# Strassen operands summed from the operand ring, stores on another queue, last products and softmax reordered

## The chip, the cores and the metric

The kernel runs on one core of one Trainium2 chip. The metric is the device time of one execution in microseconds (us); times of several executions are given by their median. PE is the matrix engine (TensorE), DVE the vector engine, ACT the scalar engine, POOL is GpSimd, and SP is the engine that issues most DMAs. Each engine takes its own instructions strictly in the order in which the program wrote them; semaphores hold an instruction back until what it needs is there.

## The reference

Three layers follow each other. First, linear attention with random features:

```
proj = x @ omega.T ;  phi(x) = exp(proj - |x|^2/2 - max) / sqrt(m)
num = phi(q) @ (phi(k).T @ v) ;  out = num / (phi(q) @ sum(phi(k)) + 1e-6)
```

Its output, as x of 2304 tokens by 512, goes into a dense mixture of four experts with given weights p: `out += p[:, e] * (relu(x @ w1[e]) @ w2[e])`, with w1[e] 512 x 1024 and w2[e] 1024 x 512. Last comes a soft mixture with 32 slots (8 experts of 4): logits `x @ phi`, a softmax over the tokens for each slot, `slot_input = d.T @ x`, two small layers for each expert, then a softmax over the slots for each token (`c`), and `out = c @ slot_out`. All is float32 to the accuracy of float32, so the kernel splits each operand into a high part (type fp32r) and a rest, and makes three products of each: high times high, high times rest, rest times high.

## The kernel before

**The dense mixture.** Its two layers are run in 24 *units*, u = 0 to 23: eight weight groups (four experts, two halves of the hidden width), each over three blocks of 768 tokens (b = u mod 3). A unit's first layer is a 2 x 2 block product. Units 0 to 2 do it plainly, in eight products (`plain1`); units 3 to 23 do it in Strassen's form with seven (`product1`, in the order I1 I2 I6 I5 I7 I3 I4). The second layer is always in Strassen's form (`product2`, seven products). A product of the first layer and one of the second alternate on PE: `product1(u, I1)`, `product2(u-1, I1)`, `product1(u, I2)`, and so on. One such product with all that is written after it is a *piece*.

**The operands.** The attention leaves x as high part and rest in DRAM (`xd`). The units take their x operands through a ring of three tiles (`xop`): `next_operand` (L457) loads the third one ahead as soon as a product is done with a tile. Strassen's form needs, for each block b, four operands that are not blocks of x but sums of such blocks (I6, I5, I7, I4). They are made once for each block and kept in DRAM (`xt`, lines 461 to 511):

- `fetch` loads high parts and rests of half a block from `xd`: four DMAs of 384 KB on SP's queue;
- `whole_again` (L472) adds the two, `block_sum` (L478) makes the four sums in place, all on DVE;
- `block_split` (L485, L487) copies the high part on ACT and subtracts it on DVE; two ticks later `keep` (L490, L491) writes both to `xt`, two DMAs on SP's queue.

`prepare(b)` puts the 18 steps of a block on a list, and every piece takes one from it (`prep_one`). Block 0 begins with unit 1, block 1 with unit 2, block 2 with unit 3, each behind what is left of the one before.

**The work between the products.** `evacuate1` takes a first-layer product out of PSUM (`u1`, `u2`, `u4`, `s1` are temporary tiles) and makes the second layer's operands, high (`split_high`, `corner_high` on ACT) and rest (`split_low` L587, `corner_low` L517 on DVE). `after(d, ...)` defers such a step to the d-th following `tick`, one of which ends each piece. For unit 23 (`hurry`) all delays from I3 on are 0. `evacuate2` adds the products of the second layer (L781) and collects them with the weights p into `x2` (L718, L720), one x2 tile for each block of tokens.

**The end.** The last group is cut into parts: letter q is a second-layer product for four of the six token tiles, r one for the other two, P a first-layer product. `SPLIT` (units 22, 23) and `ENDING` give their order; t is a task of the slot layer for a batch of four tiles: transposes (`tpm`), logits (`lq`), their sum over four partition groups and the exponentials (`slot_sum`: `lt`, L987), transposes back (`slot_back`: `dp`), `slot_gather` (`acc`), and the softmax over the slots (`slot_share1`, `slot_share2`, L1050 to L1061). During `SPLIT` each piece also takes one task off the list `side`. Behind `ENDING` the last batch is done in the open, then the hidden layer (`hq`), the second layer (`so`) and the output (`po`). The weights of the slot layer, 32 loads of 1 MB, stream in during all this; each load waits until the buffers that its place lay under are free, and the last ten take the places of the first ten.

Of the kernel before, what the change touches and what calls it, by code (L numbers as in the profile page):

```python
# [9 lines left out]
F32 = mybir.dt.float32  # L10
# [6 lines left out]
P = 128  # L17
# [23 lines left out]
def f32(ap):  # L41
    return ap.bitcast(F32)
# [3 lines left out]
def body(ctx: ExitStack, tc: tile.TileContext, ql, kl, vl, om, dp, wl, phi, w2l, out):  # L46
# [398 lines left out]
    whole = {I1: (0, 0), I2: (1, 0), I3: (1, 1)}  # L445

    def load_operand(u, i):
        b = units[u][1]
        x = xop.tile([P, 2, NP, 2 * P], F32R, name="x", tag="x")
        k = whole.get(i, i)  # L450
# [9 lines left out]

    def fetch(b, half):
        a = prep.tile([P, 2, 2 * TH], F32, name=f"xr{half}", tag=f"pre{half}")
        lo = prep.tile([P, 2, 2 * TH], F32, name="xl", tag="pre2")
        for k in range(2):
            src = xd[b][half][:, k]
            nc.sync.dma_start(out=three(a[:, k]), in_=f32(src[:, 0]))
            nc.sync.dma_start(out=three(lo[:, k]), in_=f32(src[:, 1]))
            blocks[b, (k, half)] = a[:, k], lo[:, k]
# [26 lines left out]
    prep_work = []  # L495

    def prepare(b):
        for half in range(2):
            prep_work.append(lambda half=half: fetch(b, half))
            prep_work.append(None)  # L500
            prep_work.extend(lambda kh=(k, half): whole_again(b, kh) for k in range(2))
        prep_work.extend(lambda n=n: block_sum(b, n) for n in range(4))
        for pair_ in ((I6, I5), (I7, I4)):
            prep_work.extend(lambda i=i: block_split(b, i) for i in pair_)
            prep_work.append(None)

    def prep_one():
        if prep_work:
            f = prep_work.pop(0)
            if f:  # L510
                f()

# [25 lines left out]
    def product1(u, i):  # L538
        if i in (I1, I2, I7):
            accumulator1("X" if i == I1 else "B")  # L540
        q = acc1["B" if i in (I2, I7, I4) else "X"][:, :, 0:TH]
        pass1(u, i, xs_.pop((u, i)), q, i in (I1, I2, I7))
        evacuate1(u, i, q)
        next_operand(u, i)
        weights_after(u, i)
        if u == XB and i == I1:
            prepare(u - 1)
        prep_one()
        tick()
        pump()  # L550

    def plain1(u, n):
        out = n // 2
        a, half = ((0, 0), (1, 0), (1, 1), (0, 1))[out]
        key = "XB"[out % 2]
        if n % 2 == 0:
            accumulator1(key)
        q = acc1[key][:, :, 0:TH]
        k = n % 2
        w = next(i for i, at in PLAIN.items() if at == (a, k))  # L560
        pass1(u, w, xs_[u, (k, half)], q, k == 0)
        if n in (2, 3, 6, 7):
# [6 lines left out]
        if u and n == 0:  # L569
            prepare(u - 1)  # L570
        prep_one()
        tick()
        pump()
# [23 lines left out]
    def evacuate1(u, i, q, plain=False):  # L597
# [8 lines left out]
        if u == 0:  # L606
            done.update(rd(i) for i in range(7))
        hurry = u == NU - 1
        now = (lambda n: 0) if hurry else (lambda n: n)

# [31 lines left out]
        elif i == I3:  # L642
# [7 lines left out]
            after(1, ("s2", u), second)  # L650
            after(now(1), ("h", u, I7), lambda: split_high(u, I7, q), rd(I7))
            after(now(1), ("h", u, I5), lambda: split_high(u, I5, s1), rd(I5))
# [15 lines left out]
    def rest(u, now=lambda n: n):  # L668
        L = lt_
# [5 lines left out]
        if units[u][0] == 0:  # L675
            after(1, ("s4", u), lambda: nc.vector.tensor_tensor(out=s4, in0=s4, in1=s2, op=ALU.subtract), ("s2", u))
        after(now(1), ("h", u, I6), lambda: split_high(u, I6, s2), ("s2", u), rd(I6))
        after(now(2), ("l", u, I6), lambda: split_low(u, I6, s2), ("h", u, I6))
        after(now(2), ("h", u, I3), lambda: split_high(u, I3, s4), ("s4", u), rd(I3))
        after(now(3), ("l", u, I5), lambda: split_low(u, I5, s1), ("h", u, I5))  # L680
        after(now(3), ("h", u, I4), lambda: split_high(u, I4, r22), ("r22", u), rd(I4))
        after(now(5), ("l", u, I3), lambda: split_low(u, I3, s4), ("h", u, I3))
        after(now(7), ("l", u, I4), lambda: split_low(u, I4, r22), ("h", u, I4))

# [37 lines left out]
    def product2(u, i, ps=range(NP), tags=None):  # L722
# [211 lines left out]
    def slot_tasks(b):  # L934
# [406 lines left out]
```

## Time and profile before

| | |
|---|---|
| three runs | median 1014.27 us (1012.26 to 1014.7) |
| profiled execution | 1012.07 us, of which the span from first to last instruction is 1010.2 us |
| PE busy | 960.0 us (95%) |
| DVE, ACT, POOL busy | 703.4, 502.1, 344.0 us (70%, 50%, 34%) |
| DMA on SP's queue | 231.54 MB, 66.7% of the 16 engines' span |
| mean granted clock of PE | 0.978 |

Busy shares are means over stages with different limits. A clock of 1.00 is 2.4 GHz, the lower level is 1.2 GHz; a stretch with both shows a value between. An instruction's idle time carries the name of what ended it.

### The profile page before, as it was taken

The numbers are of one execution on the slowest core, as the hardware profiler recorded it, in microseconds if no ns is written. First come the engines' busy times: TensorE is split into PE (matmuls) and PEld (weight loads), VectorE is DVE, ScalarE is ACT, GpSimd is POOL, SyncE is SP. The second block draws the span as 40 slices with busy tenths as digits, with TensorE's granted clock in tenths as the row PEclk, the third lists the DMA queues.
The fourth block names the chain that finished last, engine by engine and source line by source line (L and its number), as shares of the span: only waits on it lengthen the run. The fifth ranks groups of instructions, "written<-read, shape, count | busy, mean of one in ns | idle before, by whom it ended". The sixth has DMA issues, their size and how long they took to land.

```text
span 1010.2 us, 18116 instructions
## 1 busy us (share of the span) xinstructions
PE 960.0 (95%) x7074; PEld 914.8 (91%) x7074; DVE 703.4 (70%) x1268; ACT 502.1 (50%) x940; POOL 344.0 (34%) x288
## 2 busy tenths in 40 slices
PE   8999989997688999999999999999999999898797
PEld 8999989997688999999999999999999998786544
DVE  7888874888597767877676787667678665646422
ACT  5899883453443544445354444535544443343322
POOL 7888853142422341334134133414413240000000
PEclk9999999999799999999999999999999999797999
DMA  8688755776778565786656566665656654348995
GB/s 291 181 250 275 247 179 160 278 259 256 270 256 294 187 227 187 272 270 230 230 187 230 188 230 223 193 229 186 226 188 228 223 176 154 97 157 315 409 373 235
DMA packets 65525, 233.48 MB, mean 231 GB/s; under 512 B 8608, under 2 KB 17952, under 8 KB 61344
## 3 DMA queue, kind: packets, MB, share of 16 engines
q1 hardware_dynamic: 65152, 231.54, 66.7%
q8 instruction: 56, 0.92, 0.4%
q10 hardware_dynamic: 288, 0.79, 0.2%
q14 instruction: 29, 0.24, 0.1%
HBM read 208.71 MB, written 23.59 MB: 230 GB/s over the span
## 4 chain that ended last, share of the span: by engine, by line
PE 82%; DVE 8%; DMA 4%; ACT 3%; issue 1%; SPq 1%; ACTq 0%; POOL 0%; DVEq 0%
PE X L530 18%; PE X L738 16%; PE B L530 13%; PE B L738 12%; PE kv L220 3%; PE num L244 3%; PE Xq L738 2%; PE pj L176 2%; PE so L1201 2%; PE hq L1173 2%; PE pj L177 2%; PE pj L178 2%; PE tp L234 1%; PE Bq L738 1%; DMA xt<-xh 1%
## 5 line engine op out<-in xcount | busy, mean ns | idle before, releaser
L530 PE MATMUL X<-x,w1h 128*128 128x384 f32 x768 | 200.7, 342 | 15.1 <-ACT u L614 9.4
L530 PE MATMUL B<-x,w1h 128*128 128x384 f32 x600 | 154.2, 337 | 4.7 <-issue 2.9
L530 PEld LDWEIGHTS X<-x,w1h 128*128 128x128 f32 x768 | 137.4, 193 | 19.4 <-ACT u L614 9.8
L530 PE MATMUL X<-x,w1l 128*128 128x384 f32 x384 | 130.6, 340 | 0.0
L415 POOL TENSOR_TENSOR Tw<-raww 128x512 f32<-128x512 f32 x30 | 44.7, 1513 | 203.2 <-DMA raww<-wl 203.2
L530 PEld LDWEIGHTS B<-x,w1h 128*128 128x128 f32 x600 | 104.9, 189 | 6.2 <-issue 4.0
L530 PE MATMUL B<-x,w1l 128*128 128x384 f32 x300 | 100.4, 335 | 0.0
L601 DVE TENSOR_TENSOR u<-B,u 128x768 f32<-128x768 f32 x23 | 22.0, 957 | 101.7 <-PE B L530 101.7
L201 ACT ACTIVATE fe<-pj,nb 128x128 f32<-128x128 f32 x288 | 82.8, 389 | 10.1 <-DVE nb L194 9.3
L530 PEld LDWEIGHTS X<-x,w1l 128*128 128x128 f32 x384 | 73.6, 192 | 0.0
L429 POOL TENSOR_TENSOR w1l<-Tw,w1h 128x512 fp32r<-128x512 f32 x28 | 37.2, 1330 | 82.8 <-ACT w1h L428 82.8
L429 POOL TENSOR_TENSOR w2l<-raww,w2h 128x512 fp32r<-128x512 f32 x24 | 31.0, 1295 | 93.2 <-ACT w2h L428 93.2
L184 DVE TENSOR_REDUCE stat<-pj 128x4 f32<-128x512 f32 x72 | 49.5, 687 | 10.4 <-PE pj L178 9.6
L530 PEld LDWEIGHTS B<-x,w1l 128*128 128x128 f32 x300 | 56.3, 188 | 0.0
L429 POOL TENSOR_TENSOR w2l<-Tw,w2h 128x512 fp32r<-128x512 f32 x32 | 41.8, 1306 | 40.7 <-ACT w2h L428 40.7
L429 POOL TENSOR_TENSOR w1l<-raww,w1h 128x512 fp32r<-128x512 f32 x25 | 39.1, 1564 | 42.9 <-ACT w1h L428 42.9
L151 POOL TENSOR_TENSOR lo<-raw,hi 128x512 fp32r<-128x512 f32 x35 | 44.7, 1277 | 20.5 <-ACT hi L148 19.9
L583 ACT CAST s3h<-X 128x768 fp32r<-128x768 f32 x21 | 16.8, 802 | 67.8 <-DVE X L517 67.8
L176 PE MATMUL pj<-om_hi,hi 128*128 128x256 f32 x144 | 45.3, 315 | 1.4 <-ACT fe L201 1.1
L720 DVE SCALAR_TENSOR_TENSOR x<-B,pr,x 128x256 f32<-128x256 f32 x108 | 45.6, 478 | 1.3
L785 ACT COPY v<-X 128x768 f32<-128x768 f32 x42 | 33.7, 801 | 18.5 <-PE X L738 18.4
L178 PE MATMUL pj<-om_hi,lo 128*128 128x256 f32 x144 | 40.7, 282 | 0.8 <-POOL lo L151 0.8
(295 smaller groups left out, 3053.0 us busy)
## 6 DMA issues: line engine op xcount, KB each, us to landing
x<-xt SPq DMA_DIRECT2D x84, 768.0 KB, 4.3
x<-xd SPq DMA_DIRECT2D x75, 768.0 KB, 4.5
raww<-wl SPq DMA_DIRECT2D x16, 1024.0 KB, 7.1
w2tb<-w2l SPq DMA_DIRECT2D x11, 1024.0 KB, 8.5
raw<-ql SPq DMA_DIRECT2D x18, 512.0 KB, 4.4
xd<-xst SPq DMA_DIRECT2D x36, 256.0 KB, 2.9
raw<-kl SPq DMA_DIRECT2D x16, 512.0 KB, 5.0
w2ta<-w2l SPq DMA_DIRECT2D x5, 1024.0 KB, 6.9
```

Source lines behind the costliest of these rows:

```text
L151: (nc.gpsimd if i else nc.vector).tensor_tensor(out=lo, in0=r, in1=f32(hi), op=ALU.subtract)
L176: nc.tensor.matmul(o, lhsT=hi[:, pi, :], rhs=om_hi, start=True, stop=False)
L178: nc.tensor.matmul(o, lhsT=lo[:, pi, :], rhs=om_hi, start=False, stop=True)
L184: nc.vector.tensor_reduce(out=stats(i)[:, 4 * g:4 * g + 4, 0], in_=pjs[i, g], axis=AX.X, op=ALU.max)
L201: nc.scalar.activation(out=feats[i][:, 4 * g + h, :], in_=pjs[i, g][:, h, :], func=AF.Exp, bias=biases[i, g][:, h:h + 1], scale=1.0,)
L220: nc.tensor.matmul(kvps[b][h // 4][:, h % 4, :], lhsT=feats[i][p0:p0 + np_, h, :], rhs=v[p0:p0 + np_, h, :], start=first and h % 4 == 0, s ...
L415: nc.gpsimd.tensor_tensor(out=out_, in0=a, in1=b_, op=op)
L429: nc.gpsimd.tensor_tensor(out=lo, in0=src, in1=f32(hi), op=ALU.subtract)
L530: nc.tensor.matmul(o, lhsT=lhs[:, jp, c], rhs=rhs[:, :, k, :], start=first and not k and not n, stop=False, skip_group_check=True,)
L720: nc.vector.scalar_tensor_tensor(out=o, in0=src, scalar=w, in1=o, op0=ALU.mult, op1=ALU.add)
L738: nc.tensor.matmul(q[:, n, :], lhsT=lhs[:, jp, p, :], rhs=rhs[:, jp, :], start=i in (I1, I2, I7) and n % 2 == 0 and jp == 0 and m == 0, st ...
L785: nc.scalar.copy(out=v("v1"), in_=q)
```

## The change

Block 0 of x is still loaded from `xd`, but once, ahead of unit 1, all eight DMAs together, with the rests in the place where an x2 tile will lie. Blocks 1 and 2 are no longer loaded a second time: `whole` adds high part and rest directly from the ring's tiles while units 1 and 2 have them there. The stores to `xt` are issued by ACT. The steps stand in fixed slots: (u, 2i) is the piece of a first-layer product of unit u, (u, 2i+1) the second-layer product that follows it.

```diff
-    def fetch(b, half):
...
-    def whole_again(b, kh):
...
+    def fetch():
+        t = x2p.tile([P, 4, 2 * TH], F32, name="xl", tag="x2_1")
+        for n, (k, half) in enumerate(KH):
+            place(0, (k, half))
+            src = xd[0][half][:, k]
+            nc.sync.dma_start(out=three(blocks[0, (k, half)]), in_=f32(src[:, 0]))
+            nc.sync.dma_start(out=three(t[:, n]), in_=f32(src[:, 1]))
+            lows[k, half] = t[:, n]
...
+    def whole(b, kh):
+        if b:
+            place(b, kh)
+            hi, lo = xs_[b, kh]
+            out = three(blocks[b, kh])
+            nc.vector.tensor_tensor(out=out, in0=f32(hi), in1=f32(lo), op=ALU.add)
+        else:
+            a = blocks[b, kh]
+            nc.vector.tensor_tensor(out=a, in0=a, in1=lows[kh], op=ALU.add)
...
         def keep():
-            nc.sync.dma_start(out=f32(xt[b][i][:, 0]), in_=three(f32(hi)))
-            nc.sync.dma_start(out=f32(xt[b][i][:, 1]), in_=three(src))
+            nc.scalar.dma_start(out=f32(xt[b][i][:, 0]), in_=three(f32(hi)))
+            nc.scalar.dma_start(out=f32(xt[b][i][:, 1]), in_=three(src))
...
+        unit1 = [
+            (W, 1, KH[0]), (W, 0, KH[0]), (W, 1, KH[1]), (W, 0, KH[1]), (W, 0, KH[2]), (W, 0, KH[3]), (T, 0, 0),
+            (T, 0, 1), (W, 1, KH[2]), (T, 0, 2), (W, 1, KH[3]), (T, 0, 3), (S, 0, I5), (S, 0, I4),
+        ]
+        unit2 = [
+            (T, 1, 0), (T, 1, 1), (S, 0, I6), (S, 0, I7), (W, 2, KH[0]), (W, 2, KH[1]), (T, 1, 2), (T, 1, 3),
+            (S, 1, I6), (S, 1, I4), (W, 2, KH[2]), None, (W, 2, KH[3]), (S, 1, I5), (S, 1, I7),
+        ]
+        unit3 = [
+            None, None, *((T, 2, n) for n in range(4)), (S, 2, I6), (S, 2, I5), None, None, None,
+            (S, 2, I7), (S, 2, I4),
+        ]
```

In units 22 and 23 the steps behind I3 and I4 are deferred further (`late_` is true there, d = 1), and unit 23 has no `hurry` any more:

```diff
-            after(now(1), ("l", u, I7), lambda: split_low(u, I7, q), ("h", u, I7))
+            if not late_:
+                after(1, ("l", u, I7), lambda: split_low(u, I7, q), ("h", u, I7))
...
-            after(0, ("l", u, I2), lambda: corner_low(u, I2, q), ("h", u, I2))
-            after(0, ("s4", u), lambda: plus(pair(L["u2"]), q, pair(L["s2"]), ALU.subtract), ("s2", u))
-            rest(u, now)
+            after(2 * late_, ("l", u, I2), lambda: corner_low(u, I2, q), ("h", u, I2))
+            after(3 * late_, ("s4", u), lambda: plus(pair(L["u2"]), q, pair(L["s2"]), ALU.subtract), ("s2", u))
+            if late_:
+                x = acc1["X"][:, :, 0:TH]
+                after(3, ("l", u, I7), lambda: split_low(u, I7, x), ("h", u, I7))
+            rest(u, late_)
...
-        after(now(2), ("l", u, I6), lambda: split_low(u, I6, s2), ("h", u, I6))
+        after(2 + 2 * d, ("l", u, I6), lambda: split_low(u, I6, s2), ("h", u, I6))
```

The slot layer's tasks and the end:

```diff
-    ENDING = "q1 t q2 t q6 r1 t q5 t r2 t q7 q3 t r6 t q4 t r5 t t r7 t r3 t t r4 t t"
+    ENDING = "q1 t t q2 t q6 t q5 t q7 t q3 t q4 t t r1 r2 r6 t r5 r7 t r3 t r4"
...
-                turns[0:2], turns[2:], [], [logits], [], [total], [], [back, share1], [], [], [gather, share2],
+            tasks = [turns[0:2], turns[2:], [], [logits], [total], [], [back], [], [gather], [share1], [share2]]
...
-            tasks = [turns[0:2], turns[2:], [logits], [total], [], [back, share1], [], [gather, share2]]
+            tasks = [turns[0:2], turns[2:], [logits], [total], [], [back], [gather]]
         else:
-            tasks = [turns[0:2], turns[2:], [], [logits], [], [total]]
+            tasks = [turns[0:2], turns[2:], [logits], [total]]
...
+    slot_logits(n)
     slot_back(n - 1)
-    slot_logits(n)
+    keep_warm(4)
+    slot_sum(n)
     slot_gather(n - 1)
-    slot_sum(n)
-    slot_share1(n - 1)
-    slot_share2(n - 1)
+    keep_warm(6)
     keep_warm(10)
...
-    slot_share1(n)
-    slot_share2(n)
+    for b in (n - 2, n - 1, n):
+        slot_share1(b)
+        slot_share2(b)
```

The list `order`, which says which place each of the last layer's weights takes, is permuted: b10, c0, b9, c1, c2 come ahead of b0, b1, b2, b6.

## Rows read from the trace of the kernel before

**Rows 1.** The page: PE's busy tenths in 40 slices of the span
```profile
PE   8999989997688999999999999999999999898797
```
**Rows 2.** Stretches, one for each unit 1 to 6: length, busy us, clock, DMA share, GB/s
```profile
174.66:206.37 31.71, 31.71 (x224) 31.71 (x223) 26.43 (x33) 11.99 (x16) 8.86 (x9) 1.00 0.80 266
206.37:242.56 36.19, 33.55 (x224) 33.35 (x224) 27.06 (x36) 14.54 (x21) 10.45 (x7) 0.95 0.73 265
242.56:286.45 43.89, 32.85 (x211) 32.31 (x211) 31.71 (x36) 18.20 (x26) 13.73 (x9) 0.88 0.79 285
286.45:323.28 36.83, 30.76 (x211) 29.81 (x211) 30.48 (x40) 15.62 (x22) 6.88 (x5) 1.00 0.74 269
323.28:354.51 31.23, 31.23 (x211) 31.23 (x211) 23.46 (x33) 15.76 (x23) 13.13 (x10) 0.95 0.58 190
354.51:384.14 29.63, 29.63 (x212) 29.63 (x211) 21.22 (x29) 14.49 (x21) 12.55 (x10) 1.00 0.66 222
```
**Rows 3.** PE's waits, 206 to 330 us: total, times, longest
```profile
PE X L530 <- ACT u L614: 9.4, 2, 7.8
PE B L530 <- issue: 2.9, 1, 2.9
...
PE X L530 <- DMA x<-xd: 2.6, 1, 2.6
```
**Rows 4.** Waits of SP's queue, same stretch
```profile
SPq L490 <- ACT xh L485: 25.8, 7, 5.6
...
SPq L491 <- DVE xr L487: 13.2, 11, 2.9
```
**Rows 5.** DVE by line, 175 to 323 us: the operands' preparation
```profile
L472 DVE TENSOR_TENSOR xr<-xr,xl 128x768 f32<-128x768 f32 x12 | 14.3, 1191 | 13.2 <-DMA xl<-xd 11.6 <-issue 1.5
L487 DVE TENSOR_TENSOR xr<-xr,xh 128x768 fp32r<-128x768 f32 x12 | 14.0, 1166 | 9.8 <-ACT xh L485 9.5
```
**Rows 6.** Timeline of DVE and ACT in unit 3: start, length
```profile
256.01 2.04 DVE L587 TENSOR_TENSOR s1l<-s,s1h 128x768 fp32r<-128x768 f32 x1
...
264.42 0.95 DVE L587 TENSOR_TENSOR s4l<-u,s4h 128x768 fp32r<-128x768 f32 x1
...
265.46 0.80 ACT L614 COPY u<-X 128x768 f32<-128x768 f32 x1 [4.24 <-DVE s4l L587]
```
**Rows 7.** Timeline of ACT's queue: a DMA that it issues
```profile
1002.31 0.38 ACTq L1237 DMA_DIRECT2D out<-ob  x1
```
**Rows 8.** Three stretches of the end, columns as in Rows 2
```profile
859.46:877.76 18.30, 14.08 (x70) 11.18 (x69) 13.19 (x25) 6.87 (x12) 0.00 (x0) 0.72 0.26 86
903.55:922.05 18.50, 12.90 (x70) 10.00 (x69) 14.32 (x28) 7.17 (x13) 0.00 (x0) 0.72 0.69 265
940.95:958.81 17.86, 12.17 (x86) 7.47 (x84) 6.22 (x21) 6.50 (x17) 1.84 (x2) 0.98 1.01 422
```
**Rows 9.** Timeline of DVE behind the last first-layer product: start, length
```profile
912.22 0.42 DVE L781 TENSOR_TENSOR v<-Bq,v 128x256 f32<-128x256 f32 x1
```
**Rows 10.** Timeline of PE at the end, with idle time before and releaser
```profile
912.70 0.58 PE L738 MATMUL Bq<-w2h,e22h 128*128 128x256 f32 x1 [3.71 <-DVE v L781]
...
915.52 0.58 PE L738 MATMUL Xq<-w2h,e11h 128*128 128x256 f32 x1 [1.18 <-DVE x L720]
...
944.32 1.12 PE L975 MATMUL lt<-mo,sumr 128*128 128x512 f32 x2 [0.71 <-ACT mo L969]
...
951.16 1.53 PE L78 MATMUL warm<-om_hi 128*128 128x256 f32 x10
```
**Rows 11.** Timeline of DVE in the last batch's chain
```profile
954.05 0.28 DVE L1058 TENSOR_REDUCE cs<-lgs 128x4 f32<-128x128 f32 x1 [1.10 <-ACT lgs L1052]
...
954.99 0.22 DVE L1024 COPY d<-dp 128x64 f32<-128x64 f32 x1
```
**Rows 12.** Timelines of SP's queue and of PE: last weight load, its use
```profile
970.12 0.33 SPq L1160 DMA_DIRECT2D w2t__10988<-w2l  x1
...
997.59 1.05 PE L1201 MATMUL so<-w2t__10988,ht 128*32 128x256 f32 x16
```

More of the change, by code (lines that the diff above doesn't have):

```diff
@@ L449, in load_operand @@
         x = xop.tile([P, 2, NP, 2 * P], F32R, name="x", tag="x")
-        k = whole.get(i, i)
+        k = direct.get(i, i)
         src = xd[b][k[1]][:, k[0]] if isinstance(k, tuple) else xt[b][i]
@@ L459, in next_operand @@
             load_operand(*ring[n])
-    def fetch(b, half):
[L462 to L468, printed above, removed]
-    def whole_again(b, kh):
-        a, lo = blocks[b, kh]
-        nc.vector.tensor_tensor(out=a, in0=a, in1=lo, op=ALU.add)
-        blocks[b, kh] = a
+    KH = ((0, 0), (1, 0), (0, 1), (1, 1))
@@ new lines, in body, with place @@
+    lows = {}
+    def fetch():
[6 more added lines that the diff above has]
+            lows[k, half] = t[:, n]
+    def place(b, kh):
+        k, half = kh
+        if b == 1:
+            if kh == (0, 0):
+                stage["xr", 1] = x2p.tile([P, 4, 2 * TH], F32, name="xr", tag="x2_2")
+            blocks[b, kh] = stage["xr", 1][:, 2 * half + k]
+        else:
+            if k == 0:
+                stage["xr", b, half] = prep.tile([P, 2, 2 * TH], F32, name=f"xr{half}", tag=f"pre{half}")
+            blocks[b, kh] = stage["xr", b, half][:, k]
@@ L475, in block_sum @@
+    def whole(b, kh):
[4 more added lines that the diff above has]
+            nc.vector.tensor_tensor(out=out, in0=f32(hi), in1=f32(lo), op=ALU.add)
+        else:
+            a = blocks[b, kh]
+            nc.vector.tensor_tensor(out=a, in0=a, in1=lows[kh], op=ALU.add)
     def block_sum(b, n):
-        b11, b12, b21, b22 = (blocks[b, kh] for kh in ((0, 0), (0, 1), (1, 0), (1, 1)))
+        b11, b21, b12, b22 = (blocks[b, kh] for kh in KH)
@@ L489, in keep, with prep_steps, prep_one @@
         def keep():
-            nc.sync.dma_start(out=f32(xt[b][i][:, 0]), in_=three(f32(hi)))
-            nc.sync.dma_start(out=f32(xt[b][i][:, 1]), in_=three(src))
+            nc.scalar.dma_start(out=f32(xt[b][i][:, 0]), in_=three(f32(hi)))
+            nc.scalar.dma_start(out=f32(xt[b][i][:, 1]), in_=three(src))
         after(2, ("xt", b, i), keep)
[L495 to L511, printed above, removed]
+    def prep_steps():
+        W, T, S = whole, block_sum, block_split
+        unit1 = [
[10 more added lines that the diff above has]
+        ]
+        return {(u + 1, n): f for u, l in enumerate((unit1, unit2, unit3)) for n, f in enumerate(l) if f}
+    steps = prep_steps()
+    def prep_one(u, n):
+        if (u, n) in steps:
+            f, *a = steps.pop((u, n))
+            f(*a)
     def relu(out, in_):
@@ L545, in product1 @@
         weights_after(u, i)
-        if u == XB and i == I1:
-            prepare(u - 1)
-        prep_one()
+        prep_one(u, 2 * i)
         tick()
@@ L561, in plain1 @@
         pass1(u, w, xs_[u, (k, half)], q, k == 0)
+        prep_one(u, 2 * n)
         if n in (2, 3, 6, 7):
@@ L568, in plain1 @@
         weights_after(u, n)
-        if u and n == 0:
-            prepare(u - 1)
-        prep_one()
         tick()
@@ L607, in evacuate1 @@
             done.update(rd(i) for i in range(7))
-        hurry = u == NU - 1
-        now = (lambda n: 0) if hurry else (lambda n: n)
+        late_ = u >= NU - 2
         if i == I1 and not plain:
@@ L650, in evacuate1 @@
             after(1, ("s2", u), second)
-            after(now(1), ("h", u, I7), lambda: split_high(u, I7, q), rd(I7))
-            after(now(1), ("h", u, I5), lambda: split_high(u, I5, s1), rd(I5))
-            after(now(1), ("l", u, I7), lambda: split_low(u, I7, q), ("h", u, I7))
+            after(1, ("h", u, I7), lambda: split_high(u, I7, q), rd(I7))
+            after(1, ("h", u, I5), lambda: split_high(u, I5, s1), rd(I5))
+            if not late_:
+                after(1, ("l", u, I7), lambda: split_low(u, I7, q), ("h", u, I7))
             if plain:
@@ L663, in evacuate1, with rest @@
             after(0, ("h", u, I2), lambda: corner_high(u, I2, q), rd(I2))
-            after(0, ("l", u, I2), lambda: corner_low(u, I2, q), ("h", u, I2))
-            after(0, ("s4", u), lambda: plus(pair(L["u2"]), q, pair(L["s2"]), ALU.subtract), ("s2", u))
-            rest(u, now)
-    def rest(u, now=lambda n: n):
+            after(2 * late_, ("l", u, I2), lambda: corner_low(u, I2, q), ("h", u, I2))
[4 more added lines that the diff above has]
+            rest(u, late_)
+    def rest(u, d=0):
         L = lt_
@@ L742, in product2 @@
         evacuate2(u, i, q, ps, e, G == 0, tags)
-        prep_one()
+        prep_one(u + 1, 2 * i + 1)
         if ps[-1] == NP - 1:
@@ L925, in body @@
     x2p = pool("x2p", side="right")
+    for n in range(XB):
+        x2p.tile([P, TB, DM], F32, name=f"x2_{n}", tag=f"x2_{n}")
+    fetch()
     mp = pool("mp", side="right")
@@ L1145, in body @@
     }
-    order = ['a2', 'a3', 'a1', 'a0', 'a4', 'b9', 'b10', 'c0', 'b0', 'b1', 'b2', 'b6', 'c1', 'c2', 'b3', 'b7', 'b4', 'b5', 'b8']
+    order = ['a2', 'a3', 'a1', 'a0', 'a4', 'b10', 'c0', 'b9', 'c1', 'c2', 'b0', 'b1', 'b2', 'b6', 'b3', 'b7', 'b4', 'b5', 'b8']
     NW = NPRE + len(order)
```

25 lines of the change are left out of this document (13 added, 12 removed).

## The prediction

> **What bounds the kernel now.** I read the page's slices first [rows 1]: PE is full except in slices 10 to 14 (about 225 to 350 us) and near the end. So I cut the first place by units [rows 2]. Unit 1 takes 31.71 us without a gap, which is the price of a plain unit; unit 6 takes 29.63 us, the price of a Strassen unit. Units 2 to 5 take 36.19, 43.89, 36.83 and 31.23 us, that is 4.5, 14.3, 7.2 and 1.6 us too much: **27.5 us** are lost there. They begin where the operands of blocks 0 to 2 are prepared and end with that work. Then PE's own waits [rows 3] say what ended last: ACT's copy of a product into u2 (two waits, 9.4 us, one of 7.8), a ring load (2.6), and others of 2.6 to 2.9 us. The rest of the 27.5 us is matmuls at 1.2 GHz behind the gaps: the granted clock is 0.95, 0.88 and 0.95 in units 2, 3 and 5.
>
> Two queues stand behind these waits. SP stood 25.8 us for a copy of ACT and 13.2 us for a subtraction of DVE before it could issue stores [rows 4], and ring loads are queued behind those stores. And DVE is late: in unit 3 a subtraction takes 2.04 us where others take 0.95, s4l is done only at 265.37, and ACT's copy waits 4.24 us for it [rows 6].
>
> For the end I price a matmul by the steady unit, 29.63 us / 212 = 0.14 us. The stretches behind the last two first-layer phases hold 70 matmuls each, 9.8 us, but last 18.30 and 18.50 us at a clock of 0.72 [rows 8]: **8.5 and 8.7 us** lost. PE waits for DVE there (3.71 and 1.18 us, [rows 10]). The stretch from the last r to the hidden layer holds 86 matmuls, 12.0 us, and lasts 17.86 us: 5.8 us lost in a chain of small steps.
>
> **Preparation: DVE's load.** Nothing is saved on DVE: 12 sums, 12 differences and 12 subtractions remain, 1.05 to 1.2 us each [rows 5]. They move. By the timeline units 1 to 4 held 9, 9, 8 and 10 of these 36; now they hold 14, 14, 8 and 0. With 1.1 us each, DVE's busy time [rows 2] becomes 26.4 + 5.5 = 31.9, 27.1 + 5.5 = 32.6, 31.7, and 30.5 - 11 = 19.5 us. Units 1 to 3 thus want 96.2 us of DVE in 31.7 + 31.7 + 29.6 = 93.0 us of PE. A backlog of some us into unit 4 is certain, and harmless there.
>
> **Preparation: what goes.** Sixteen loads of 384 KB and their places in SP's queue go. So does the wait for their landing (11.6 us of DVE's idle time, [rows 5]). The eight loads that stay are issued together ahead of unit 1, behind the same stores as before. The first pair lands no earlier than before, and the next ring load is put behind four more pieces: at 422 GB/s 4 x 0.93 = 3.7 us, at unit 1's 266 GB/s 5.9 us. Its product is some 6 us further on, so I cost it nothing (bounds 0 and 2 us). Unit by unit I expect to remain:
> - Unit 2: the ring load's wait (2.6 us plus slow clock) shrinks to 0.5 us. A load now also waits for the sum that reads its tile, one DVE backlog later (bounds 0 and 2.6).
> - ACT's stores: 24 issues at 0.38 us [rows 7] are 9 us of ACT, which is 12 to 18 us busy in a unit of 30, so beside other work. But a store makes ACT wait for DVE's subtraction, and behind it ACT's copies out of PSUM are queued. The 11 waits of L491 were 13.2 us, the longest 2.9 [rows 4]. Two pieces, 31.7 / 15 x 2 = 4.2 us, lie between order and store, so most are hidden: I take 1.1 us (bounds 0 and 13.2).
> - Unit 3: the first wait for PSUM (2.9 us) becomes 1.3: as many DVE steps stand before s3l as now, but DVE comes less late. The wait of 7.8 us: slots 0 and 1 are empty, but two of the new differences stand before s4l, and POOL's weight sums slow them as now. I take 5 us and 1.9 us of slow clock (bounds 0 and 10.5, all of today's).
> - Unit 4 and 5: no preparation is left, 0.7 us for the backlog (bounds 0 and 8.8).
>
> Sum 0.5 + 1.1 + 1.3 + 5 + 1.9 + 0.7 = 10.5 us remain, so **17.0 us** are gained (bounds 27.5 and, with all upper bounds, a loss of 11).
>
> The Trainium skill ("Trainium Kernel Development and Optimization", section "Key Constraints") says that DMAs issued from SP's, ACT's and POOL's queues all run on the same 16 DMA engines, and that issuing from several only saves the issuer's time. By that rule alone moving the stores would gain nothing on the path. [Rows 4] show more than issue time: SP's queue stood 39 us for other engines with loads behind. No row yet shows stores on ACT.
>
> **The last first-layer phases.** In front of v (done at 912.64, [rows 9]) DVE does e12l, s4, s2l and s1l, 0.95 us each. PE's r4 waits for v until 912.70, and q1 until 915.52 for the collection behind s3l. With `late_` only e12l stays in front of r3's collection; s4 and s3l follow, s2l and s1l come after r4. By these lengths v is done at about 909 and q1 can start at 911.4 instead of 915.52, both at full clock. The first stretch goes alike, except that the task `back` stands behind P4 at once, so PE waits about 1.2 us for ACT's exponentials. I get 6.6 us from the first stretch and 7.2 from the second (bounds 0 and 8.5, 0 and 8.7). If the deferred steps were late, the next to wait would be P1, for s3l; its margin is about 0.3 us. s4h and s4l are needed nine pieces on.
>
> **The chain to the hidden layer.** Batch 3's transposes, logits and sum now lie ahead of r4, about 3.2 us of PE. From the end of its last sum (945.44, [rows 10]) to the hidden layer (958.81) it is 13.4 us now. The softmax of batch 3 leaves it: DVE waited 1.10 us for ACT and did four steps before it copied d at 954.99 [rows 11], 1.3 us. Ten more warm-up matmuls, 1.5 us [rows 10], stand before the same transposes. So 13.7 us, of which 0.8 lies beside r4: 17.86 becomes 12.9 us, idle time of 0.6 us ahead of it goes, 3.2 are added: **2.4 us** gained (bounds -2 and 5.8). The three softmaxes now stand behind rtot, about 2 us each on DVE, while PE has 64 matmuls of the hidden layer, 8 us; 2 us of cover are left. If that is gone, PE waits for the difference.
>
> Weights: the last load was issued at 970.12; ten of 1 MB at 422 GB/s take 24.8 us from the first use of their places, and the last is used at 997.59 [rows 8, 12], about 6 us after landing. The stream moves forward with the r products, so it does not bind. If the places came free only after r4, it would cost under 1 us.
>
> **Sum.** 1012.07 us of the profiled execution (span 1010.2) - 17.0 - 6.6 - 7.2 - 2.4 = 978.9. The median of the runs is 2.2 us above that execution: **981 us**.
>
> **Rivals.**
> - *DVE is the bound of units 2 and 3.* For it: 96 us wanted in 93. Against: it was as full in unit 1 (26.4 of 31.7 plus waits for loads) without a gap of PE. Units 2 and 3 keep their 18.7 us, only 8.8 are gained: 981 + 8.2 = 989 us.
> - *The end's wait is only renamed.* `back` ahead of r7 makes DVE stand for the transposes with r7's evacuation behind, and PE's clock falls as now. Then the two stretches give 2 us each: 981 + 9.8 = 991 us. For it: the chain through ACT is as long as before. Against: four DVE steps, 3.8 us, leave the place ahead of v [rows 9].
> - *The stores don't leave the path.* The ring loads were slow for the traffic (265 to 285 GB/s, DMA share up to 0.79, [rows 2]) and still share the engines with the stores. Then only the ring wait of 2.6 us goes: 981 + 14.4 = 995 us. Against: unit 1 runs without a gap at a share of 0.80.
> - *ACT stands at its stores (slower).* Each of the 12 store pairs holds ACT's copies out of PSUM until DVE has subtracted. It decides from a hold of 4.2 us, the two pieces. If DVE were late at each by the longest wait seen, 7.8 us [rows 3], PE would lose 12 x 3.6 = 43 us: 981 + 43 = 1024 us. Against: the longest wait of that kind was 2.9 us.
>
> **Chances.** 981 us as worked out, within 970 to 988: 0.56. DVE the bound 0.17, the end renamed 0.12, stores on the path 0.05: all faster. ACT's stores or another new stall, slower: 0.07. No change left over, within 0.3% (what a measurement of this kernel can tell): 0.03. So faster 0.90, same 0.03, slower 0.07. The range reaches from most of the 27.5 us and the end's 23 us gained (968) to the third rival with some stalls more (1001).
>
> **What would show it.** Units 2 to 5 in stretches: 33, 38, 30 and 30 us; DVE over 90% busy in units 1 to 3 and under 70% in unit 4; no wait of PE for a ring load above 1 us; in unit 3 one wait of about 5 us for u2. No store on SP's queue. At the end r4 follows r3 without a wait for v, and the clock stays at 1.00. I am wrong if PE waits for copies of ACT that stand behind its stores, if unit 3 still takes over 42 us, or if the stretch from r4 to the hidden layer is not under 15 us.

## The result and the profile after

The changed kernel takes 988.77 us (median of four runs, 985.5 to 989.22) against 1013.43 us for the kernel before on the same chip: a ratio of 0.9749 (95% interval 0.9724 to 0.9775). The profiled execution is the fastest of the four, 985.5 us with a span of 983.6 us. Forecast were 981 us, and the band given as "as worked out", 970 to 988 us, ends just below the measured time. Of the 33.2 us that were to go from the span, 26.6 went.

PE in 40 slices, beside [rows 1]: the hole of slices 10 to 13 is down to two slices of 8.

```profile
PE   8999999998899999999999999999999999998897
```

Units 2 to 5 as stretches, columns as in [rows 2]:

```profile
206.68:247.30 40.62, 34.84 (x224) 33.83 (x223) 34.71 (x47) 18.32 (x26) 9.05 (x6) 0.92 0.54 195
247.30:282.17 34.87, 30.15 (x212) 29.77 (x212) 29.90 (x38) 18.56 (x27) 14.10 (x10) 1.00 0.83 283
282.17:311.80 29.63, 29.63 (x213) 29.63 (x211) 22.86 (x32) 12.61 (x18) 6.47 (x5) 1.00 0.81 277
311.80:341.43 29.63, 29.63 (x212) 29.63 (x211) 21.95 (x29) 15.42 (x22) 13.14 (x10) 1.00 0.56 188
```

Units 4 and 5 have the price of a Strassen unit and unit 3 lost 9 us less, but unit 2 is 4.4 us *longer* than before. PE's waits there, as in [rows 3]:

```profile
PE X L765 <- ACT v L814: 4.5, 1, 4.5
PE B L558 <- issue: 2.6, 1, 2.6
PE X L558 <- ACT u L637: 2.2, 1, 2.2
...
```

The first is new. The second ends at 254.24 us, just behind DVE's s3l (done at 254.14), and is called the wait for s3l below. ACT's queue at that place (start, length, idle time before and what ended it):

```profile
223.07 0.33 ACTq L514 DMA_DIRECT2D xt<-xr  x1
223.44 0.62 ACT L428 CAST w1h<-Tw 128x512 fp32r<-128x512 f32 x1 [1.26 <-DVE xr L510]
223.51 0.36 ACTq L513 DMA_DIRECT2D xt<-xh  x1
226.97 0.33 ACTq L514 DMA_DIRECT2D xt<-xr  x1
227.34 0.80 ACT L814 COPY v<-X 128x768 f32<-128x768 f32 x1 [3.29 <-DVE xr L510]
```

An issue costs 0.33 us, as [rows 7] let expect. But the second of L514's stores stands from 223.9 to 226.97 us until DVE has subtracted (L510), and the copy of the product at 227.34 stands behind it. PE needs that copy and starts again at 228.19, and its next product takes 4.01 us, at a clock of 0.50, instead of 2.15. And DVE, in the same stretch:

```profile
185.76 0.96 DVE L492 TENSOR_TENSOR xr<-xr,xl 128x768 f32<-128x768 f32 x1 [3.19 <-DMA xl<-xd]
...
217.28 2.04 DVE L611 TENSOR_TENSOR s2l<-s,s2h 128x768 fp32r<-128x768 f32 x1
...
220.98 2.05 DVE L510 TENSOR_TENSOR xr<-xr,xh 128x768 fp32r<-128x768 f32 x1
...
226.00 0.95 DVE L510 TENSOR_TENSOR xr<-xr,xh 128x768 fp32r<-128x768 f32 x1
...
234.00 0.96 DVE L510 TENSOR_TENSOR xr<-xr,xh 128x768 fp32r<-128x768 f32 x1 [0.99 <-ACT xh L508]
```

It stands 3.19 us for the landing of block 0's first rest, and then works from 185.76 to 233 us without a pause. In unit 3 the same late DVE holds ACT's copy u2, with two differences (L497) ahead of s4l, as in [rows 6]:

```profile
262.27 1.02 DVE L497 TENSOR_TENSOR xr<-xr 128x768 f32<-128x768 f32 x1
263.22 0.94 DVE L611 TENSOR_TENSOR s4l<-u,s4h 128x768 fp32r<-128x768 f32 x1
...
264.27 0.80 ACT L637 COPY u<-X 128x768 f32<-128x768 f32 x1 [5.08 <-DVE s4l L611]
```

The three stretches of the end that answer to [rows 8] (the second now holds eight transposes, 1.0 us, that stood behind it):

```profile
846.76:858.08 11.32, 10.02 (x70) 8.49 (x69) 9.75 (x17) 5.42 (x9) 0.00 (x0) 1.00 0.37 131
884.38:896.90 12.52, 10.43 (x78) 8.62 (x77) 10.89 (x21) 6.11 (x12) 0.00 (x0) 1.00 0.75 296
917.20:933.47 16.27, 13.18 (x85) 8.68 (x83) 5.09 (x16) 4.53 (x13) 1.84 (x2) 0.90 1.01 421
```

The first two lost over three tenths of their length, and the clock stays at 1.00 there. The third, from r4 to the hidden layer, is still 16.27 us, at a clock of 0.90. PE in it:

```profile
921.63 0.64 PE L992 MATMUL lq<-x2t,phis 128*32 128x256 f32 x8 [1.53 <-ACT x2t L984]
...
924.78 1.51 PE L1062 MATMUL acc<-x,d 128*32 128x512 f32 x8
927.16 2.16 PE L78 MATMUL warm<-om_hi 128*128 128x256 f32 x16 [0.88 <-DVE mo L1068]
929.26 0.31 PE L1044 MATMUL dp<-ident,mo 32*128 32x32 f32 x2
```

The gain by the start times of equal work in both traces (unit 6, P4 and q2 in the two last units, hidden layer, end); 0.4 and 0.5 us are what the work ahead of the two P4 became longer:

| stretch | forecast | measured |
|---|---|---|
| units 2 to 5 | 17.0 | 13.4 (148.14 - 134.75) |
| first stretch | 6.6 | 6.6 (18.30 - 11.32, less 0.4) |
| second stretch | 7.2 | 6.5 (18.50 - 12.52, less 0.5, with the 1.0 of the transposes) |
| from there to the hidden layer | 2.4 | -0.8 |
| hidden layer to the end | 0 | 1.2 (51.39 - 50.13, at a clock of 0.97 instead of 0.93) |
| start of unit 1 | 0 | -0.3 |
| sum | 33.2 | 26.6 |

### The profile page after: what moved, and what is told of

The parts are those of the page before. It is cut to its first block, busy times and chain, and to the rows that moved or that the text cites. A ratio compares the mean times of both kernels' runs of the same rounds, so it can differ in the third digit from the quotient of the medians.

```text
span 983.6 us, 18106 instructions
## 1 busy us (share of the span) xinstructions
PE 950.3 (97%) x7084; PEld 907.2 (92%) x7084; DVE 700.5 (71%) x1268; ACT 501.3 (51%) x940; POOL 344.0 (35%) x288
## 4 chain that ended last, share of the span: by engine, by line
PE 85%; DVE 8%; ACT 3%; DMA 2%; issue 1%; SPq 1%; ACTq 0%; DVEq 0%
PE X L558 19%; PE X L765 17%; PE B L558 14%; PE B L765 12%; PE kv L220 3%; PE num L244 3%; PE Xq L765 2%; PE pj L176 2%; PE so L1230 2%; PE pj L177 2%; PE pj L178 2%; PE tp L234 2%; PE Bq L765 1%; PE hq L1202 1%; DMA xl<-xd 1%
## 5 line engine op out<-in xcount | busy, mean ns | idle before, releaser
L558 PE MATMUL X<-x,w1h 128*128 128x384 f32 x768 | 196.5, 336 | 2.2 <-ACT u L637 2.2
L558 PEld LDWEIGHTS X<-x,w1h 128*128 128x128 f32 x768 | 134.4, 189 | 4.3 <-ACT u L637 2.4
L558 PE MATMUL X<-x,w1l 128*128 128x384 f32 x384 | 128.5, 335 | 0.0
## 6 DMA issues: line engine op xcount, KB each, us to landing
w2tb<-w2l SPq DMA_DIRECT2D x11, 1024.0 KB, 13.4
```

Source lines behind the costliest of these rows:

```text
L558: nc.tensor.matmul(o, lhsT=lhs[:, jp, c], rhs=rhs[:, :, k, :], start=first and not k and not n, stop=False, skip_group_check=True,)
```

## The experiments

All are edits of the changed kernel, and all ratios are to the kernel before.

**Which half gives what.** One kernel has only the preparation, one only the end (`late_`, SPLIT's tasks, ENDING, the last chain).

```diff
 only the preparation:
-    ENDING = "q1 t t q2 t q6 t q5 t q7 t q3 t q4 t t r1 r2 r6 t r5 r7 t r3 t r4"
+    ENDING = "q1 t q2 t q6 r1 t q5 t r2 t q7 q3 t r6 t q4 t r5 t t r7 t r3 t t r4 t t"
...
 only the end:
-    def prep_steps():
+    prep_work = []
...
```

> The preparation alone: fetch, sums from the ring, slots and ScalarE's stores as in the changed kernel, the end (late_, ENDING, tasks, softmaxes, weight order) as before. Theory (two independent parts; the traces put 13.4 us of the gain into units 2 to 5 and 13.5 us behind them): 1013.4 - 13.4 = 1000 us, unit 2 takes 40.6 us, unit 3 34.9, units 4 and 5 29.6. Rival (the parts need each other, for instance because the weight stream or the clock at the end decides): under 5 us or over 20 us gained, 1008 or 993 us.

> The end alone: late_, ENDING, tasks, softmaxes at the end and weight order as in the changed kernel, the preparation as before. Theory (independent parts): 1013.4 - 13.5 = 1000 us, the two stretches behind the last first-layer phases without a wait for v, units 2 to 5 as before (36, 44, 37, 31 us). Rival (the parts need each other): the gains of this run and of the preparation alone do not add up to the 25 us, by more than 4 us.

The preparation alone: 1000.25 us, ratio 0.9887 (0.9862 to 0.9913). The end alone: 996.72 us, 0.9854 (0.9831 to 0.9876). The gains of 1.13 and 1.46% add up to 2.59%, and the whole gains 2.51% (2.25 to 2.76), so within the noise the halves don't touch each other. The first trace has the three waits again (4.55, 2.56 and 2.73 us), with units 2 and 3 at 39.8 and 37.0 us. In the second the stretch from the last r to the hidden layer takes 14.74 us at a clock of 1.00: 1.5 of the 16.27 us above are a lower clock behind the wait of 1.53 us. It is not in each execution: of the nine traces with the same matmuls there, four take 14.74 or 14.75 us at a clock of 1.00, and five take 16.05 to 16.35 us at 0.89 or 0.90.

**The stores on SP's queue again.**

```diff
-            nc.scalar.dma_start(out=f32(xt[b][i][:, 0]), in_=three(f32(hi)))
-            nc.scalar.dma_start(out=f32(xt[b][i][:, 1]), in_=three(src))
+            nc.sync.dma_start(out=f32(xt[b][i][:, 0]), in_=three(f32(hi)))
+            nc.sync.dma_start(out=f32(xt[b][i][:, 1]), in_=three(src))
```

> The changed kernel, only the 24 stores to xt issued by SP's queue again. Theory A (in unit 2 ScalarE stands at a store until DVE has subtracted, and its copy v is queued behind: 4.5 us of wait and 2.6 us of slow clock): that wait of PE goes, unit 2 falls from 40.6 to 33 to 36 us, the time to about 983 us; SP's loads stand behind the stores, with some us of margin. Rival B (DVE's backlog is the bound whichever queue stores): unit 2 stays at 39 us or more because now a ring load comes late, 988 us or more.

986.66 us, 0.9756 (0.9734 to 0.9778): nothing. Unit 2 takes 39.2 us. The longest of its waits, units 1 to 5, then SP's queue, DVE and PE at that place:

```profile
PE X L558 <- DMA x<-xd: 4.0, 1, 4.0
...
```

```profile
222.37 0.32 SPq L514 DMA_DIRECT2D xt<-xr  x1
...
227.04 1.82 DVE L489 TENSOR_TENSOR xr<-x 128x768 f32<-128x768 f32 x2
...
228.05 0.32 SPq L453 DMA_DIRECT2D x<-xd  x1
...
233.43 1.01 PE L558 MATMUL X<-x,w1h 128*128 128x384 f32 x2 [4.04 <-DMA x<-xd]
```

ACT's wait of 4.5 us is gone and a ring load's of 4.0 us stands in its place, as rival B had it. The stores did not hold this load up: the last of them had gone at 222.37 us, and SP's queue stood 5.3 us more, until DVE had done the sum (L489) that still reads the load's tile. In the changed kernel the same sum begins at 227.73 and the load follows at 228.8 us; PE, held by ACT until 228.19, needs it only at 236.75 and doesn't wait. DVE is late either way, and it shows at the first of its consumers that PE comes to. The Trainium skill ("Trainium Kernel Development and Optimization", section "Key Constraints") says that issuing from several queues saves only the issuer's time; by that rule moving the stores gains nothing, and these two kernels agree (0.9749 and 0.9756).

**Without the twelve differences.** The kernel leaves out `block_sum`, so the operands are not the right ones.

```diff
-        return {(u + 1, n): f for u, l in ... for n, f in enumerate(l) if f}
+        return {(u + 1, n): f for u, l in ... for n, f in enumerate(l) if f and f[0] is not T}
```

> The changed kernel without the twelve differences of block_sum on DVE (the operands that Strassen's form needs are then the blocks themselves, so units from 3 on compute something else); stores, sums of high part and rest, and subtractions stay. Theory (DVE's backlog of 96 us of work in 93 us is behind both the hold at ScalarE's stores in unit 2 and the waits of unit 3): 12 us less on DVE, the 14.1 us lost in units 2 and 3 fall under 4 us, about 977 us. Rival (ScalarE's stores cost by themselves, by issue time and by the landing that later copies wait for): unit 2 still loses over 5 us, 985 us or more.

979.06 us, 0.9683 (0.9662 to 0.9703). Units 2 and 3:

```profile
206.25:239.28 33.03, 31.99 (x224) 31.67 (x223) 26.28 (x36) 17.38 (x25) 8.54 (x6) 1.00 0.63 225
239.28:273.80 34.52, 31.64 (x212) 31.26 (x211) 26.12 (x34) 18.57 (x27) 13.29 (x10) 0.95 0.83 285
```

With 8.4 us less on DVE in unit 2, 7.6 of its 8.9 lost us are back. ACT's hold is DVE's lateness. The theory wanted the loss of units 2 and 3 under 4 us; 6.2 us stayed, 4.9 of them in unit 3, where the wait for s3l is still 2.55 us: it has another cause (the other slots, next).

**Later stores; other slots.** In one kernel block 0's stores are queued four pieces after their order; in the other the last splits of block 1 stand a slot earlier and block 2's steps behind s4l.

```diff
 later stores:
-        after(2, ("xt", b, i), keep)
+        after(2 if b else 4, ("xt", b, i), keep)
...
 other slots:
-            (S, 1, I6), (S, 1, I4), (W, 2, KH[2]), None, (W, 2, KH[3]), (S, 1, I5), (S, 1, I7),
+            (S, 1, I6), (S, 1, I4), (W, 2, KH[2]), (W, 2, KH[3]), (S, 1, I5), (S, 1, I7),
...
-            None, None, *((T, 2, n) for n in range(4)), (S, 2, I6), (S, 2, I5), None, None, None,
-            (S, 2, I7), (S, 2, I4),
+            *[None] * 6, *((T, 2, n) for n in range(4)), (S, 2, I6), (S, 2, I5),
...
+        unit4 = [*[None] * 4, (S, 2, I7), (S, 2, I4)]
...
```

> Theory: in unit 2 ScalarE stands because a store is queued two pieces after its subtraction was ordered, and VectorE is later than that. With the stores of block 0 queued four pieces after (8 us), the 4.54 us gap at 228 us and the slow clock behind it go: unit 2 from 40.6 to 33 to 35 us, unit 3 as it is (34.9), time 979 to 982 us against 985 to 988. Rival: VectorE's backlog is the bound whichever way it shows (as when SyncE stored: its ring load then waited 4.04 us); then the gap moves on to a ring load or to an accumulator, unit 2 stays at 38 to 40 us, and the time at 985 to 988 us.

> Theory: both waits of unit 3 are places in VectorE's queue, not its sum of work. Block 1's last two splits go one slot earlier, into VectorE's idle 2.1 us at 243 us, and block 2's four differences and four splits stand behind s4l instead of in front of it, the last two in unit 4. The first wait goes from 2.55 to 0 to 1 us, the second from 2.17 to 0, and unit 3 from 34.9 to 30 to 31 us; unit 2 keeps its 4.5 us gap (40.6). Time 981 to 984 us. Rival: the work is only moved and shows again in unit 4, which then takes 32 to 34 us instead of 29.6; time as before this edit, 985 to 988 us.

984.87 us, 0.9719 (0.9665 to 0.9773), and 986.07 us, 0.9735 (0.9687 to 0.9783): neither differs from the change by more than the intervals. Units 2 to 4 take 38.0, 36.6 and 29.6 us in the first and 41.9, 34.5 and 31.6 us in the second. The waits of the first, units 1 to 5, and then of the second:

```profile
PE B L558 <- issue: 2.6, 1, 2.6
PE X L558 <- DMA x<-xd: 2.4, 1, 2.4
PE X L558 <- ACT u L637: 2.3, 1, 2.3
...
```

```profile
PE X L765 <- ACT v L814: 4.5, 1, 4.5
PE X L558 <- ACT u L637: 1.8, 1, 1.8
PE B L558 <- DVE s3l L611: 1.8, 1, 1.8
PE B L558 <- issue: 1.6, 1, 1.6
...
```

Both rivals held in the main: one place mended, the wait shows at the next. Later stores take ACT's wait away, and the ring load comes late, because the sums that free its tile stand in DVE's queue. The other slots show that the two splits were what stood ahead of s3l: the 2.55 us of unit 3 are 0.6 us. But 1.57 us came up at the same place of unit 4, and unit 2 is no shorter.

**Other engines.** GpSimd does the twelve differences; ScalarE scales the first products into x2; and the latter with the later stores and without the warm-up matmuls (next).

```diff
-        nc.vector.tensor_tensor(out=out_, in0=a, in1=b_, op=ALU.subtract)
+        nc.gpsimd.tensor_tensor(out=out_, in0=a, in1=b_, op=ALU.subtract)
...
-            nc.vector.tensor_scalar_mul(o, src, w)
+            nc.scalar.activation(out=o, in_=src, func=AF.Copy, scale=w)
```

> The twelve differences of the preparation run on GpSimd instead of VectorE. Theory: VectorE loses 12 x 1.1 = 13 us of work in units 1 to 3 and the waits of unit 2 go as when the differences were left out: unit 2 at 33 to 35 us, unit 3 at 33 to 35 us, time 979 to 981 us. Rival: GpSimd takes some 2 us for each, and VectorE's operations of two inputs take twice as long while it runs (2.04 us instead of 0.95 us in the trace), so that VectorE loses about as much as it gains: units 2 and 3 stay at 38 to 41 and 34 to 37 us, time 985 to 990 us.

> ScalarE instead of VectorE scales the first products into x2 (12 operations in each of units 0 to 2). Theory: the waits of units 2 and 3 are VectorE's sum of work, as when the twelve differences were left out; here it loses 12 x 0.42 = 5.1 us in each of units 0 to 2 (three of them take 1.27 us), 10 us in units 1 and 2 against 13 us there. Unit 2 goes from 40.6 to 33 to 36 us, unit 3 from 34.9 to 33 to 35 us: 979 to 982 us. Rival: ScalarE is the engine that stood; every one of these operations makes it wait for VectorE's addition into the accumulator and holds its copies behind. Then unit 2 stays at 38 to 42 us and units 1 and 3 get waits of their own: 985 to 992 us.

> Three edits together: ScalarE scales the first products into x2, block 0's stores are queued four pieces after their order instead of two, and the sixteen warm-up matmuls are left out. If the three add up: unit 2 at 32 to 34 us, unit 3 at 33 to 35 us, 1.5 us less ahead of the hidden layer: 976 to 979 us. If ScalarE is the engine that stands, the longer delay of the stores does not help and it comes to 983 to 990 us.

989.12 us, 0.9749 (0.9689 to 0.9809); 988.72 us, 0.9757 (0.9732 to 0.9782); 984.68 us, 0.9719 (0.9693 to 0.9744). The rivals held for the first two, and the third came out where it was to if ScalarE stands. On GpSimd a difference takes 2.35 us, and DVE pays while it runs (line, count, busy us, mean ns, units 1 to 3; in the changed kernel these two are 13.8 us, 1154 ns, and 2.8 us, 949 ns):

```profile
L510 DVE TENSOR_TENSOR xr<-xr,xh 128x768 fp32r<-128x768 f32 x12 | 15.8, 1325 | 7.1 <-ACT xh L508 7.1
...
L611 DVE TENSOR_TENSOR s4l<-u,s4h 128x768 fp32r<-128x768 f32 x3 | 5.5, 1817 | 0.0
```

Over the whole execution DVE is busy for 698.4 us instead of 700.5. In the second PE waits 6.2 us for ACT's v (two times) and 4.7 for u2: DVE has 14 us less to do (686.7 us busy for 700.5), but ACT's scalings in units 1 to 3 wait 24.1 us for DVE's additions (L808) ahead of them.

**Without the sixteen warm-up matmuls** ahead of the last transposes.

```diff
-    keep_warm(6)
-    keep_warm(10)
```

> The sixteen warm-up matmuls ahead of the last transposes are left out (they compute nothing). Theory: they wait for the collection of batch 2's sum (idle 0.88 us) and keep the transposes, whose exponentials are done at 926.1, until 929.26; without them the transposes start at 926.5 and the hidden layer 2.7 to 3 us earlier: 982 to 985 us. Rival: they hold the clock; without them the granted clock falls to its lower level behind the 2 to 3 us gap, the 40 small matmuls to the hidden layer (3.4 us) take twice as long, and with some of the hidden layer's 64 (7.1 us) nothing is gained or up to 4 us are lost: 985 to 992 us.

985.47 us, 0.9725 (0.9678 to 0.9773), not told apart by time. In the trace the hidden layer starts 589.80 us after unit 6 instead of 592.04, and the clock, down in the gathering, is up again ahead of it:

```profile
925.55 1.89 PE L1062 MATMUL acc<-x,d 128*32 128x512 f32 x8
927.37 0.31 PE L1044 MATMUL dp<-ident,mo 32*128 32x32 f32 x2
928.33 0.62 PE L78 MATMUL warm<-om_hi 128*128 128x256 f32 x3 [0.65 <-DVE mo L1068]
928.87 1.05 PE L1133 MATMUL acc<-x,d 128*32 128x512 f32 x4
```

So the sixteen cost 2.2 us here, a little under the theory's 2.7. The two other kernels without them (the three edits together, above, and the last experiment) agree: from r4 to the hidden layer 12.40 and 12.39 us at a clock of 1.00, against 14.74 with the sixteen at that clock. They hold nothing up that is worth it.

**The old due times** at the end (no `late_`), with the new order of products and tasks.

```diff
-        late_ = u >= NU - 2
+        hurry = u == NU - 1
+        now = (lambda n: 0) if hurry else (lambda n: n)
...
```

> The changed kernel with the old due times of the last two first-layer phases (no `late_`): the splits s1l, s2l, s4 and s4l stand ahead of v again; the new order of the last products and tasks stays. Theory (the forecast's): the deferral gives most of the two stretches, 6.6 and 5.7 us, since four steps of 0.95 us leave VectorE's queue ahead of v and the granted clock stays up: 995 to 1000 us. Rival: the order of the tasks gives it (transposes, logits and sums no longer between the last r products); then the stretches keep over half of the gain: 987 to 992 us.

995.14 us, 0.9828 (0.9796 to 0.9859), at the lower edge of what the theory had. The two stretches, and PE's waits in them:

```profile
847.52:861.84 14.32, 10.09 (x70) 8.46 (x69) 11.89 (x21) 7.04 (x12) 0.00 (x0) 1.00 0.29 103
888.03:905.87 17.84, 12.56 (x78) 10.31 (x77) 13.91 (x27) 8.31 (x15) 0.00 (x0) 0.81 0.83 334
```

```profile
PE acc L1059 <- DVE d L1049: 5.7, 2, 3.9
...
```

The deferral is worth 3.0 and 5.3 us of the two stretches. In the second that is most of the gain, as the theory had it; in the first, 4.0 of the 7.0 us are there without the deferral and belong to the other edits of the end, so there the rival, the new order, is the larger part. Without it DVE's copy of d, 0.28 us long, stands behind the splits, and PE waits for that instead of v.

**The same steps in the order that the waits asked for**, and the sixteen warm-up matmuls left out.

```diff
-        after(2, ("xt", b, i), keep)
+        after(2 if b else 3, ("xt", b, i), keep)
...
-            (W, 1, KH[0]), (W, 0, KH[0]), (W, 1, KH[1]), (W, 0, KH[1]), (W, 0, KH[2]), (W, 0, KH[3]), (T, 0, 0),
...
+            (W, 1, KH[0]), None, (W, 1, KH[1]), *((W, 0, kh) for kh in KH), (T, 0, 0), (W, 1, KH[2]),
...
-            (T, 1, 0), (T, 1, 1), (S, 0, I6), (S, 0, I7), (W, 2, KH[0]), (W, 2, KH[1]), (T, 1, 2), (T, 1, 3),
...
+            (T, 1, 0), (T, 1, 1), (W, 2, KH[0]), (S, 0, I6), (S, 0, I7), (W, 2, KH[1]), (T, 1, 2), (T, 1, 3),
...
+            *[None] * 6, *((T, 2, n) for n in range(4)),
...
+        unit4 = [*[None] * 4, (S, 2, I6), (S, 2, I5), None, None, (S, 2, I7), (S, 2, I4)]
...
-    keep_warm(6)
-    keep_warm(10)
```

> The same steps in another order, by what the waits showed, and without the sixteen warm-up matmuls. VectorE stood 3.19 us for block 0's low half at 182.57 us and then worked without a pause until 233 us; block 0's sums now stand two slots later, behind work that is ready. Block 2's first sum stands ahead of block 0's last splits, so that the ring's tile comes free; block 0's stores are queued three pieces after their order; block 1's last splits stand one slot earlier; block 2's differences stand behind s4l and its splits in unit 4. Theory (places in the queue decide, since VectorE's sum of work in units 1 to 4, 115.7 us, fits in their 122.7 us of products): unit 2 from 40.6 to 32 to 35 us, unit 3 from 34.9 to 30 to 32 us, unit 4 stays at 29.6, 1.5 us less ahead of the hidden layer: 974 to 979 us. Rival (the sum of work with GpSimd's slowing decides): each wait shows again one place on, units 2 to 4 take 102 to 105 us together as now (105.1): 983 to 986 us.

977.23 us, 0.9655 (0.9621 to 0.969): faster than both kernels. Units 2 to 4, and DVE at the place of the 3.19 us:

```profile
207.02:238.72 31.70, 31.70 (x223) 31.70 (x223) 31.46 (x39) 17.39 (x25) 10.99 (x6) 1.00 0.69 233
238.72:275.00 36.28, 31.98 (x212) 31.29 (x211) 29.02 (x38) 15.86 (x23) 14.47 (x11) 0.95 0.68 245
275.00:305.92 30.92, 29.79 (x212) 29.61 (x211) 22.87 (x31) 15.05 (x20) 3.70 (x4) 1.00 0.82 286
```

```profile
187.79 0.95 DVE L492 TENSOR_TENSOR xr<-xr,xl 128x768 f32<-128x768 f32 x1
```

Unit 2 runs without a gap although DVE is busy for 31.46 of its 31.70 us. Units 2 to 4 take 98.9 us instead of 105.1, below the rival's 102. Of the gain over the changed kernel some 6 us are theirs, and 2.2 to 2.4 us are the warm-up matmuls'. Unit 3 is the theory's miss: 36.3 us, not 30 to 32, with waits of 0.8 us for a split of GpSimd, 1.6 us for s3l and 1.9 us for u2 left; unit 4 takes 30.9, not 29.6. How much of unit 2's gain is due to each of the three edits there was not tried.

## Why the prediction was off by 8 us, step by step

- **Units 2 to 5, 17.0 forecast, 13.4 measured.** The step that failed is the term of the stores in unit 2: "Two pieces, 31.7 / 15 x 2 = 4.2 us, lie between order and store, so most are hidden: I take 1.1 us". The second split of unit 2 was done at 226.95 us, some 11 us after the product of its slot, and the store behind it cost PE 4.54 us of wait and 2.2 us of lower clock in the two pieces behind: the mechanism of the rival "ACT stands at its stores", at one place instead of twelve. Behind it is the same lateness that the forecast looked at only where it ended: "A backlog of some us into unit 4 is certain, and harmless there". It was harmless there, but a queue served in order makes each step late by the backlog of that moment. The sum of DVE's work in units 1 to 4 was right (115.7 us, forecast and measured), its place was not: 28.2, 34.7, 29.9 and 22.9 us instead of 31.9, 32.6, 31.7 and 19.5. By the trace the lateness began with DVE's 3.19 us for a landing, which the forecast counted as gone together with the old loads, and grew where DVE met GpSimd (2.04 and 2.05 us instead of 0.95); no run takes that landing out alone.
- Unit 2's other 2.0 us, waits for DVE's s3l (0.48) and s2l (0.76) and what went with them, were not in the sum.
- The ring load: 0.5 forecast, none measured, but it is the next in line (4.0 us with the stores on SP, 2.4 us with later stores), for the reason given: a load "now also waits for the sum that reads its tile".
- Unit 3: the wait for s3l 1.3 forecast, 2.55 measured; u2 5 and 1.9 forecast, 2.17 and 0.5 measured. Units 4 and 5: 0.7 forecast, none.
- That the four units together are off by only 3.6 us is luck: unit 2 lost 7.3 us more than the terms for it, unit 3 lost 3.0 us less, units 4 and 5 0.7 us less. That the rival "DVE is the bound" priced the time at 989 us is luck too: it wanted 18.7 us lost in units 2 and 3 where 14.1 were, and nearly half of what the forecast lacks in the span comes from the chain. Unit 2 of the last experiment, full of DVE's work and without a gap, speaks against it.
- **The stretches** came near the forecast, 6.6 and 6.5 us for 6.6 and 7.2. The reason given, fewer splits ahead of v, is shown for the second; without the deferral PE waits for d, though, and not for v. In the first the deferral is 3.0 us only, and which of the other edits gives the rest was not tried. `back` cost 1.22 and 1.42 us for ACT, as the 1.2 forecast.
- **The chain** failed by 3.2 us; 12.9 us were forecast for 16.27. 1.5 us of that are the lower clock. New are a wait of 0.57 us for r4's collection and one of 0.88 us for the collection ahead of the warm-up matmuls, and the wait for ACT's copy of the transposes is 1.53 us where it was 1.02. The ten more warm-up matmuls cost about what was forecast, 1.4 us for 1.5 (0.74 + 2.16 - 1.53, by their lengths at the higher clock).
- From the span to the median it was 3.3 - 2.2 = 1.1 us more than forecast: the profiled execution was a quick one. Three other kernels with the same preparation (the first experiment, the one without warm-up matmuls and the one with the old due times) show unit 3 at 36.9 to 37.1 us, and not at 34.87.
- The three softmaxes beside the hidden layer made no wait of PE, as forecast.
- Two of the three signs of being wrong came true: PE waits for a copy of ACT that stands behind a store, and the stretch from r4 to the hidden layer is not under 15 us (14.74 us in the executions at a clock of 1.00). DVE was to be over 90% busy in units 1 to 3 and under 70% in unit 4; it was 85 to 89% and 77%.
- Two readings of the prediction are a little off: in [rows 1] the hole ends with slice 13, and the upper bounds of the preparation add up to a loss of about 10 us, not 11.

## What to carry to other kernels

A DMA that waits for an engine stops what stands behind it on the engine that issues it: here a store made a PSUM copy wait 3.29 us. Moving it to another queue took that wait away and gained nothing, because the engine that was late then showed at its next consumer; the cure is to have the operand ready when the DMA is issued. When an in-order engine is nearly full, as DVE was here at 85 to 89%, look for the first moment at which it stands for something late while ready work is queued behind, and put that work in front: here the same steps in another order gave some 6 us more. Count an engine's lateness at the time of each consumer, not as a sum at the end.

## What was not expected of the hardware

DVE's operations of two SBUF operands that met one of GpSimd did not run at half speed; they stood until GpSimd's was over. GpSimd in the changed kernel, beside DVE's two long operations shown above:

```profile
216.69 1.81 POOL L429 TENSOR_TENSOR w1l<-Tw,w1h 128x512 fp32r<-128x512 f32 x1 [11.46 <-ACT w1h L428]
220.12 2.10 POOL L429 TENSOR_TENSOR w1l<-Tw,w1h 128x512 fp32r<-128x512 f32 x1 [1.61 <-ACT w1h L428]
```

The split of 217.28 us met the first, 216.69 to 218.50, and ended 0.82 us behind it; the subtraction of 220.98 met the second, 220.12 to 222.22, and ended 0.81 us behind it, each about the 0.95 us that such an operation takes alone. The Trainium skill ("SBUF — State Buffer", section "SBUF: two separate sides") says that the port pair which the two share is locked for a whole instruction and the loser blocks; the trace agrees. This fits what the twelve differences on GpSimd gave: they took 28 us there and freed 11.7 us of DVE, some 8.5 us of which came back in units 1 to 3 as longer operations of DVE, and nothing was gained.
